# One pool for the eight PSUM banks of a banded attention, and another order of its first two blocks

## The chip, the cores and the metric

The kernel runs on one core of one Trainium2 chip. It is one program; the metric is its device time in microseconds, the median of several executions. TensorE (PE) multiplies matrices and writes PSUM, which has eight banks; VectorE (DVE) and ScalarE (ACT) read PSUM and compute element by element, GpSimd (POOL) computes between tiles of SBUF, and SyncE (SP) issues most of the DMAs. Each engine works through its own queue in order, and an instruction that needs another engine's result waits on a semaphore.

## The reference

Attention over 4 batches of 8 heads, 768 positions of 64 dimensions, in which each position sees the first 4 positions (the sinks) and the last 128 of its own. Then a mixture of 8 experts over 3072 tokens of 512 dimensions, each expert with 1024 hidden units, weighted by a table that is normalized in eight Sinkhorn steps:

```python
keep = is_sink | in_window                   # n_sink = 4, window = 128
scores = np.where(keep, scale * (q @ k.T), -1e9)
a = np.exp(scores - scores.max(-1, keepdims=True))
a = a / (a.sum(-1, keepdims=True) + 1e-9)
x = (a @ v)                                  # regrouped to (3072, 512)
P = np.exp(x @ w_gate - max)                 # 8 times: rows, columns to sum 1, times N / E
for e in range(E):
    out += P[:, e:e + 1] * (np.maximum(x @ w1[e], 0) @ w2[e])
```

All of it is in fp32. The kernel splits the operands of the large products into a high and a low part and adds three products of parts.

## The kernel before, in words

The attention stage takes blocks of 128 positions, 24 in all (4 batches of 6). Half a block, four heads, is a unit; unit j is half j % 2 of block j // 2, so that the fifth unit has number 4. The work of a unit goes as follows. `transpose_qk` (L451) turns k and q by four transposes on PE into one PSUM bank. `split_qk` copies that bank to the high part on ACT (L460) and takes the low part on DVE (L461); in a batch's second block a small copy of the sinks follows on DVE (L464). `scores` (L483) multiplies them in 12 matmuls into four banks, one bank per head. `exponential` handles one head: on DVE a predicated copy that brings the two pieces of the window together (L492, not in a batch's first block), then the sum with the mask and the scaling (L493), and on ACT the exponential (L495). `scaled` has the reciprocals of the sums on DVE (L501, L502) and the scaling of four heads on POOL (L504). `transpose_p` (L514) turns the weights into a bank and `copy_p` copies them on ACT (L520) and masks a copy on POOL (L522). `values` (L564) multiplies with v into a bank called O, which both halves of a block share; `split_p`, `small_products` and `sink_values` (L537, L538, L544, L549, L572) add the sinks' part. `store_x` copies O half by ACT (L581) and half by DVE (L582), issues the DMA to DRAM, and for the first 1024 tokens queues a high copy on ACT (`behind`, L589) and a low part on POOL (`lows`, L590). `gate_products` (L597) computes the gate's logits of a block, and ACT copies them (L599).

Beside attention runs a filling, `fill`, that is a generator of steps of the first expert's products for a third of the tokens. `plain_g1` is 12 matmuls of 256 columns into a bank (L631) in two steps; ACT (L636) and DVE (L637) read that bank. `plain_g2` is 12 matmuls of 512 columns (L646) in four steps; ACT (L654) or DVE (L656) reads the bank. The DVE instruction is not emitted at once: it is put on the list `pending` and emitted by the next `flush`. `next_piece` copies a piece of a weight on ACT (L749) and puts its low part (L750) on the same list. `run_fill(k)` emits k steps.

The whole stage stands in `tc.manual_schedule()`: every engine's queue has the order in which the program emits the instructions. The first two blocks, up to the fifth unit's sums, are written out by hand, with `idle(k)`, k matmuls of zeros into a bank of their own, in places. Then a list `rounds` rules. Each round emits the scores and sums of the units `new_s` (two units in most rounds, a half in the first three), `ahead` filling steps, the values of the units of the round before, the gate's products, the q/k transposes of `new_qk`, the P transposes of `new_p`, the small products, `store_x`, and then `steps` filling steps. What is pending on DVE is flushed behind the second head's sums. From block 4 on, a round with four filling steps has two `plain_g1` or one `plain_g2`, by turns. In the last rounds no scores are left.

PSUM banks are given out by `new_bank`. It keeps a ring of eight numbers, `banks`; a tile takes the first number, which goes to the end of the ring at once, or, with `keep`, only when the program appends it again: O does so in the written-out part (`store_x` appends it), and the bank of zeros until the fourth round. A tile whose bank is still being read waits for the readers. The framework's planner, which lays out all semaphores ahead of the run, resolves the waits. In a pool with `bufs=8` and one name the planner itself picks the bank, among those that no tile holds any more.

## Time and profile before

| | us |
|---|---|
| median of 3 runs (lowest, highest) | 2114.72 (2113.69, 2117.1) |
| the profiled execution | 2114.56 |
| its span | 2112.8 |
| PE busy in the span | 2073.9 (98%) |
| DVE, ACT, POOL busy | 1478.3, 842.9, 703.9 |

The profiled execution stands for the others: it is 0.16 us from the median, and 1.8 us of it lie around the span. Times below are microseconds from the start of the span. In a timeline row the first number is the start, the second the duration; a bracket at the end gives the idle time before the instruction on its engine and what ended it. xN is the number of instructions in the row.

### The profile page before, as it was taken

To read this page: it belongs to the slowest core of one execution; us is meant where nothing else is said; L and a number is where in the kernel's file an instruction comes from. 1 tells how busy PE (TensorE), PEld (TensorE's weight loads), DVE (VectorE), ACT (ScalarE), POOL (GpSimd) and SP (SyncE) were. 2 spreads that over 40 slices of the span, in tenths; PEclk is the share of its full clock that TensorE was granted. 3 is DMA by queue.
4 is the path that set the end of the run, shared out by engine and by line. 5 is a ranking of instruction groups with operands and counts; after the bars stand their busy time and mean duration, and the time that the engine had idled before them with its cause. 6 is when DMAs were issued, how large, how long until landed. Compare 5 with 4: busy or idle time off the path is not lost.

```text
span 2112.8 us, 31704 instructions
## 1 busy us (share of the span) xinstructions
PE 2073.9 (98%) x10609; PEld 1721.6 (81%) x10609; DVE 1478.3 (70%) x2770; ACT 842.9 (40%) x1799; POOL 703.9 (33%) x829
## 2 busy tenths in 40 slices
PE   8998899999999999999999999999999999999998
PEld 6787787888888888888888888888888888888887
DVE  6766778877877776856666666666666666666666
ACT  6766635444444444443322332322433322332322
POOL 5665533242332321322322223223322332223223
PEclk9999999999999999999999999999999999999999
DMA  6644329999898996786666666668766666666662
GB/s 141 156 106 103 75 90 350 298 305 300 294 313 286 306 296 209 239 270 199 208 191 205 204 201 197 204 200 299 263 199 197 203 205 192 205 200 192 204 198 85
DMA packets 397624, 453.82 MB, mean 215 GB/s; under 512 B 99664, under 2 KB 265744, under 8 KB 396560
## 3 DMA queue, kind: packets, MB, share of 16 engines
q1 hardware_dynamic: 397064, 451.57, 68.7%
q8 instruction: 87, 1.43, 0.3%
q14 instruction: 81, 0.66, 0.1%
q10 hardware_dynamic: 392, 0.16, 0.0%
HBM read 314.17 MB, written 137.46 MB: 214 GB/s over the span
## 4 chain that ended last, share of the span: by engine, by line
PE 93%; DVE 4%; ACT 2%; DMA 1%; issue 1%; POOL 0%; SPq 0%; DVEq 0%; ACTq 0%; POOLq 0%
PE c L968 41%; PE o L1532 20%; PE held L1532 8%; PE o L1218 7%; PE held L1218 7%; PE st L646 2%; PE st L631 2%; PE st L564 2%; PE st L483 1%; DVE sc L493 1%; DVE st L492 1%; PE st L451 1%; PE st L514 1%; ACT KQ L460 0%; ACT sc L495 0%
## 5 line engine op out<-in xcount | busy, mean ns | idle before, releaser
L994 ACT CAST hf<-w 128x512 fp32r<-128x512 f32 x448 | 265.2, 621 | 562.2 <-POOL w L1499 299.7
L1532 PE MATMUL o<-hf,W2q 128*128 128x512 f32 x1920 | 472.0, 389 | 0.0
L1532 PEld LDWEIGHTS o<-hf,W2q 128*128 128x128 f32 x1920 | 360.0, 188 | 75.5 <-DVE acc L1546 0.9
L968 PE MATMUL c<-T,W1q 128*128 128x512 f32 x1530 | 388.9, 389 | 0.2 <-DVE w L1480 0.2
L997 DVE TENSOR_TENSOR hf<-w,hf 128x512 fp32r<-128x512 f32 x448 | 329.4, 764 | 76.4 <-ACT hf L994 68.9
L968 PEld LDWEIGHTS c<-T,W1q 128*128 128x128 f32 x1530 | 286.8, 188 | 60.7 <-DVE w L1480 0.9
L1546 DVE TENSOR_TENSOR acc<-o,acc 128x512 f32<-128x512 f32 x298 | 204.8, 688 | 170.0 <-PE o L1532 170.0
L968 PE MATMUL c<-B,W1q 128*128 128x512 f32 x1134 | 278.3, 389 | 0.0
L968 PEld LDWEIGHTS c<-B,W1q 128*128 128x128 f32 x1134 | 212.6, 188 | 44.0
L1499 POOL TENSOR_TENSOR w<-w 128x512 f32<-128x512 f32 x64 | 82.7, 1292 | 493.2 <-DVE w L1481 493.2
L1480 DVE TENSOR_TENSOR w<-c,M 128x512 f32<-128x512 f32 x192 | 132.4, 689 | 139.7 <-PE c L968 135.3
L1476 ACT COPY M<-c 128x512 f32<-128x512 f32 x192 | 112.9, 588 | 250.4 <-PE c L968 250.3
L1532 PE MATMUL held<-hf,W2q 128*128 128x512 f32 x768 | 195.1, 390 | 0.7 <-DMA W2q<-w2s 0.7
L1218 PE MATMUL held<-W2f,h 128*128 128x512 f32 x672 | 171.1, 390 | 0.0
L968 PE MATMUL c<-T,W1f 128*128 128x512 f32 x672 | 171.0, 390 | 0.1
L1218 PE MATMUL o<-W2f,h 128*128 128x512 f32 x672 | 170.6, 390 | 0.1
L1532 PEld LDWEIGHTS held<-hf,W2q 128*128 128x128 f32 x768 | 143.9, 188 | 30.9 <-DMA W2q<-w2s 1.1
L1514 POOL TENSOR_TENSOR w<-w 128x512 f32<-128x512 f32 x64 | 106.3, 1660 | 176.1 <-DVE hf L997 176.1
L1218 PEld LDWEIGHTS o<-W2f,h 128*128 128x128 f32 x672 | 126.0, 188 | 27.0 <-DVE acc L1225 0.9
L968 PEld LDWEIGHTS c<-T,W1f 128*128 128x128 f32 x672 | 125.9, 188 | 26.6 <-issue 0.5
L1218 PEld LDWEIGHTS held<-W2f,h 128*128 128x128 f32 x672 | 125.9, 188 | 26.4 <-DVE W2f L997 0.5
L1503 POOL TENSOR_TENSOR w<-w 128x512 f32<-128x512 f32 x64 | 83.7, 1308 | 176.0 <-DVE w L1481 171.8
(212 smaller groups left out, 2714.8 us busy)
## 6 DMA issues: line engine op xcount, KB each, us to landing
W2q<-w2s SPq DMA_DIRECT2D x448, 256.0 KB, 3.0
W1q<-w1s SPq DMA_DIRECT2D x444, 256.0 KB, 2.9
w1s<-W1f SPq DMA_DIRECT2D x56, 896.0 KB, 7.6
w2s<-WT SPq DMA_DIRECT2D x136, 256.0 KB, 4.0
r<-in_moe_w_dram SPq DMA_DIRECT2D x64, 512.0 KB, 4.0
w2s<-W2f SPq DMA_DIRECT2D x56, 256.0 KB, 5.1
PB<-psd SPq DMA_DIRECT2D x16, 512.0 KB, 3.7
w2s<-W2f SPq DMA_DIRECT2D x56, 128.0 KB, 6.7
```

Source lines behind the costliest of these rows:

```text
L564: nc.tensor.matmul(O[r * D:(r + 1) * D, c], lhsT=x_[:, 2 * c + r], rhs=y_[:, 2 * c + r], start=(j == 0 and c == 0), stop=(j == len(ops) - ...
L968: nc.tensor.matmul(ps, lhsT=w1(a, k), rhs=x[:, b, k, :], start=(start and j == 0), stop=(stop and j == len(TERMS) - 1), skip_group_check=n ...
L994: nc.scalar.copy(dst[:, 0], src)
L997: low_ = nc.vector.tensor_sub(dst[:, 1], src, f32(dst[:, 0])).ins
L1218: nc.tensor.matmul(o, lhsT=h[c, th][:, a, off:off + P], rhs=W2F[n][:, w, c, :], start=(begin and c == 0 and j == 0), stop=(end and c == 1 ...
L1476: nc.scalar.copy(t, T["c2"])
L1480: nc.vector.tensor_add(w, T["c1"], T[m])
L1499: nc.gpsimd.tensor_sub(S3, T["A11"], T["A21"])
L1503: nc.gpsimd.tensor_add(T["A21"], T["A21"], T["A22"])
L1514: at(k, lambda: nc.gpsimd.tensor_sub(T["A11"], w, T["A11"]))
L1532: nc.tensor.matmul(o, lhsT=W2Q[part, n, m][:, a, k * P:(k + 1) * P], rhs=F[part, n, H_OF[m]][:, w, :], start=(j == 0 and (begin or not hol ...
L1546: nc.vector.tensor_add(sums[m, k], o, sums[m, k])
```

## The change

`new_bank` becomes a pool of eight buffers with one name, and the ring, `keep` and the appending go. `split_qk` is divided into its ACT part, `high_qk`, and its DVE part, `low_qk`. In the written-out part the DVE parts move behind sums that stood after them, the sums of two or four heads are brought together, `store_x(0)`, `next_piece`, `high` and `total(3)` change places with transposes and copies, and one of the four low parts of x goes to DVE. The first four filling steps, so far in the first round (`ahead` 4), are emitted ahead of it, behind the fifth unit's sums. The filling's steps per round are 4 in all rounds but two of the steady part (m is 11 and 17, with none), and 4 in three of the last four, where they were 2, 2, 0 and 0: the sum is 92 steps before and after.

```diff
@@ -367,16 +367,8 @@
     w1r_ = ctx.enter_context(ExitStack())
     w1r = right(w1r_, "w1r", 1)
     ph = ctx.enter_context(ExitStack())
-    ps_a = ph.enter_context(tc.tile_pool(name="ps_a", bufs=1, space=PSUM))
-    banks = list(range(8))
-
-    def new_bank(shape, keep=False):
-        j = banks.pop(0)
-        if not keep:
-            banks.append(j)
-        t = ps_a.tile(shape, F32, name=f"st{j}")
-        return (t, j) if keep else t
-
+    ps_a = ph.enter_context(tc.tile_pool(name="ps_a", bufs=8, space=PSUM))
+    new_bank = lambda shape: ps_a.tile(shape, F32, name="st")
     wa, rawp = right(ph, "wa", 2), right(ph, "rawp", 2)
     XF["B12"] = b12p.tile([P, 2, KH, HT], F32R, name="B12")
     ab = ctx.enter_context(ExitStack())
@@ -451,17 +443,29 @@
                 nc.tensor.transpose(pt[:, 2 * pr + j, :], r[:, h0 + 2 * pr:h0 + 2 * pr + 2, :].rearrange("p h d -> p (h d)"), ident)
                 idle(gap * (pr == j == 0))
 
+    def qk_parts(m, hh):
+
+        t = KQ[hh]
+        return (t[:, w, :, SINK:].rearrange("p r (a c) -> p r a c", a=2)[:, :, :, turn_of(*spans[m])] for w in range(2))
+
+    def high_qk(m, hh):
+
+        nc.scalar.copy(next(qk_parts(m, hh)), us[m]["qk", hh].rearrange("p (r a) t -> p r a t", a=2))
+
+    def low_qk(m, hh):
+
+        b, i = spans[m]
+        hi, lo = qk_parts(m, hh)
+        nc.vector.tensor_sub(lo, us[m]["qk", hh].rearrange("p (r a) t -> p r a t", a=2), f32(hi))
+        if i == 1:
+
+            t = KQ[hh]
+            nc.vector.tensor_copy(t[:, :, :, 0:SINK], f32(t[:, :, :, place(b, 0)])[:, :, :, 0:SINK])
+
     def split_qk(m, hh):
 
-        b, i = spans[m]
-        t = KQ[hh]
-        hi, lo = (t[:, w, :, SINK:].rearrange("p r (a c) -> p r a c", a=2)[:, :, :, turn_of(b, i)] for w in range(2))
-        src = us[m]["qk", hh].rearrange("p (r a) t -> p r a t", a=2)
-        nc.scalar.copy(hi, src)
-        nc.vector.tensor_sub(lo, src, f32(hi))
-        if i == 1:
-
-            nc.vector.tensor_copy(t[:, :, :, 0:SINK], f32(t[:, :, :, place(b, 0)])[:, :, :, 0:SINK])
+        high_qk(m, hh)
+        low_qk(m, hh)
 
     def scores(m, hh):
 
@@ -550,11 +554,11 @@
         for j, (t, ls) in enumerate(sums):
             nc.vector.tensor_copy(Pt[:, t, :], tsk[:, 1 + j, 0:E])
 
-    def values(m, hh, keep=True):
+    def values(m, hh):
 
         u = us[m]
         if hh == 0:
-            u["O"], u["bank"] = new_bank([P, KC, P], True) if keep else (new_bank([P, KC, P]), None)
+            u["O"] = new_bank([P, KC, P])
         O = u["O"]
         ops = list(zip(u["V"], u["PT"]))
         c0 = hh * NP
@@ -574,8 +578,6 @@
 
     def store_x(m):
         b, i = spans[m]
-        if us[m]["bank"] is not None:
-            banks.append(us[m]["bank"])
         tok = b * S + i * P
         xr = us[m]["xr"] = att.tile([P, KC, P], F32, name="xr")
         nc.scalar.copy(xr[:, 0:NP], us[m]["O"][:, 0:NP])
@@ -587,7 +589,7 @@
                 x_ = xr[:, kh * KH:(kh + 1) * KH, :]
                 b_ = xblock(kh, tok // HT)
                 behind.append(lambda b_=b_, x_=x_, cols=cols: nc.scalar.copy(b_[:, 0, :, cols], x_))
-                lows.append(lambda b_=b_, x_=x_, cols=cols: nc.gpsimd.tensor_sub(b_[:, 1, :, cols], x_, f32(b_[:, 0, :, cols])))
+                lows.append(lambda b_=b_, x_=x_, cols=cols, eng=nc.gpsimd: eng.tensor_sub(b_[:, 1, :, cols], x_, f32(b_[:, 0, :, cols])))
         later.append((tok // P, xr))
 
     def gate_products(t, xr):
@@ -755,11 +757,11 @@
     pieces.extend([(0, 0), (1, 0), (0, 1), (1, 1)])
     rounds = []
     for n in range(FIRST, 2 * HALF + 1):
-        rounds.append(([n + 1], {4: [6], 5: [7, 8]}.get(n, [n + 3]), [n], (4, 0) if n == FIRST else (0, 2), 2))
+        rounds.append(([n + 1], {4: [6], 5: [7, 8]}.get(n, [n + 3]), [n], (0, 0) if n == FIRST else (0, 2), 2))
     rounds.append(([2 * HALF + 2, 2 * HALF + 3], [2 * HALF + 4, 2 * HALF + 5], [2 * HALF + 1], (0, 4), 2))
     for m in range(HALF + 1, L + 3):
         both = lambda j: [2 * j, 2 * j + 1] if j < L else []
-        rounds.append((both(m + 1), both(m + 2), both(m), (0, {L - 1: 2, L: 2, L + 1: 0, L + 2: 0}.get(m, 4)), 2))
+        rounds.append((both(m + 1), both(m + 2), both(m), (0, 0 if m > L + 1 or m in (11, 17) else 4), 2))
     at_block = lambda m: len(rounds) - (L + 3 - m)
     waiting = []
     load_kq(0)
@@ -770,21 +772,18 @@
     load_v(1)
     nc.sync.dma_start(wgp[:, :, 0:E], wg.rearrange("(k p) e -> p k e", p=P))
     load_plain_raw(1, 0)
-    zeros = new_bank([P, P], True)
+    zeros = new_bank([P, P])
 
     def idle(k_):
         for _ in range(k_):
-            nc.tensor.matmul(zeros[0], lhsT=zero, rhs=zero, start=True, stop=True)
-
-    turn_p, score, value, copied_p, cast_qk, total = ((lambda j, f=f: f(*divmod(j, 2))) for f in (transpose_p, scores, values, copy_p, split_qk, scaled))
+            nc.tensor.matmul(zeros, lhsT=zero, rhs=zero, start=True, stop=True)
+
+    turn_p, score, value, copied_p, cast_qk, cast_high, cast_low, total = (
+        (lambda j, f=f: f(*divmod(j, 2))) for f in (transpose_p, scores, values, copy_p, split_qk, high_qk, low_qk, scaled))
 
     def exps(j, *hs):
         for h in hs:
             exponential(j // 2, j % 2 * HH + h)
-
-    def low():
-        while lows:
-            lows.pop(0)()
 
     def high():
         while behind:
@@ -801,13 +800,13 @@
         score(1)
         transpose_qk(1, 0)
         transpose_qk(1, 1)
-        cast_qk(2)
+        cast_high(2)
         mask_sinks(0)
-        exps(1, 0, 1)
+        exps(1, 0, 1, 2, 3)
         total(0)
-        exps(1, 2, 3)
+        cast_low(2)
         value_step(0)
-        cast_qk(3)
+        cast_high(3)
         idle(5)
         score(2)
         exps(2, 0)
@@ -815,60 +814,61 @@
         turn_p(0)
         copied_p(0)
         exps(2, 1)
+        cast_low(3)
         idle(3)
         value(0)
         turn_p(1)
-        exps(2, 2)
+        exps(2, 2, 3)
         copied_p(1)
         value_step(1)
         score(3)
-        exps(2, 3)
         load_kq(3)
         load_kq(4)
         load_plain_raw(0, 1)
         load_plain_raw(1, 1)
-        next_piece()
         exps(3, 0, 1)
         total(2)
-        exps(3, 2)
+        exps(3, 2, 3)
         idle(2)
         value(1)
-        store_x(0)
-        exps(3, 3)
-        flush(len(pending))
-        high()
-        total(3)
         transpose_qk(2, 0)
         turn_p(2)
+        total(3)
         copied_p(2)
+        store_x(0)
+        next_piece()
+        high()
         split_sinks(0)
         split_p(1, slice(0, H))
-        next_piece()
-        idle(5)
+        flush(len(pending))
+        idle(6)
         turn_p(3)
         copied_p(3)
-        cast_qk(4)
-        flush(len(pending))
+        next_piece()
         value(2)
         small_products(1, [])
         load_v(2)
-        idle(2)
+        idle(1)
         value(3)
         sink_values(1)
+        cast_qk(4)
+        flush(len(pending))
         store_x(1)
         high()
         score(4)
         transpose_qk(2, 1)
         load_kq(5)
-        low()
-        add_up_rows()
+        for j in range(3):
+            lows.pop(0)()
         exps(4, 0, 1)
+        lows.pop(0)(eng=nc.vector)
         cast_qk(5)
         exps(4, 2, 3)
         total(4)
+        add_up_rows()
+        run_fill(4)
+        flush(len(pending))
         for n, (new_s, new_qk, new_p, (ahead, steps), np_) in enumerate(rounds):
-            if n == 3:
-                banks.append(zeros[1])
             if n in (at_block(4), at_block(5)):
                 load_plain_raw(n - at_block(4) + 2, 0)
             elif n in (at_block(6), at_block(7)):
@@ -907,7 +907,7 @@
             run_fill(ahead)
             flush(len(pending))
             for j in waiting:
-                values(*divmod(j, 2), j + 1 not in waiting)
+                values(*divmod(j, 2))
             old = list(summed)
             summed.clear()
             for g in later:
```

## Rows read from the trace of the kernel before

**Rows 1.** The page, busy time: engine, us (share of the span), instructions

```profile
PE 2073.9 (98%) x10609; PEld 1721.6 (81%) x10609; DVE 1478.3 (70%) x2770; ACT 842.9 (40%) x1799; POOL 703.9 (33%) x829
```

**Rows 2.** Windows by stage: from:to, length, busy us (instructions) per engine, clock, DMA share, GB/s

```profile
29.00:63.65 34.65, 29.91 (x246) 24.93 (x244) 26.93 (x103) 23.26 (x78) 18.73 (x45) 0.85 0.44 94
63.65:275.00 211.35, 189.97 (x2038) 165.20 (x2037) 141.73 (x632) 142.79 (x490) 119.74 (x257) 1.00 0.46 105
275.00:2112.80 1837.80, 1829.75 (x8137) 1512.13 (x8129) 1293.34 (x1957) 660.83 (x1182) 549.41 (x480) 1.00 0.72 230
```

**Rows 3.** Waits of PE, 63.65 to 275: us in total, times, longest

```profile
PE st L631 <- DVE xr L582: 9.4, 7, 1.8
PE st L483 <- DVE h L637: 8.6, 10, 0.9
...
PE st L483 <- DVE acc L656: 1.1, 1, 1.1
```

**Rows 4.** Timeline of PE in three rounds

```profile
156.69 1.70 PE L483 MATMUL st<-KQ 64*128 64x260 f32 x24
158.32 1.09 PE L564 MATMUL st<-PT,vr 128*64 128x128 f32 x16
...
186.16 1.65 PE L631 MATMUL st<-B,W 128*128 128x256 f32 x12
189.37 1.69 PE L631 MATMUL st<-B,W 128*128 128x256 f32 x12 [1.56 <-DVE xr L582]
190.99 1.47 PE L483 MATMUL st<-KQ 64*128 64x260 f32 x19
193.33 0.62 PE L483 MATMUL st<-KQ 64*128 64x260 f32 x5 [0.87 <-DVE h L637]
193.88 0.66 PE L564 MATMUL st<-PT,vr 128*64 128x128 f32 x8
...
207.84 3.08 PE L631 MATMUL st<-B,W 128*128 128x256 f32 x24
```

**Rows 5.** Timeline of ACT, the copy of the gate's bank

```profile
186.26 0.24 ACT L599 COPY ls<-st 128x128 f32<-128x128 f32 x1
```

**Rows 6.** Timeline of DVE, the round of 190.99

```profile
192.09 0.30 DVE L493 CUSTOM_DVE_ANT_0 sc<-st,mask 128x132 f32<-128x132 f32 x1
...
192.64 0.29 DVE L493 CUSTOM_DVE_ANT_0 sc<-st,mask 128x132 f32<-128x132 f32 x1
...
199.91 0.42 DVE L582 COPY xr<-st 128x256 f32<-128x256 f32 x1
```

**Rows 7.** Timeline of PE, fifth to ninth unit

```profile
27.82 0.99 PE L483 MATMUL st<-KQ 64*128 64x260 f32 x12
...
31.00 0.39 PE L483 MATMUL st<-KQ 64*128 64x260 f32 x2 [1.60 <-ACT KQ L460]
...
32.52 4.63 PE L631 MATMUL st<-B,W 128*128 128x256 f32 x24
...
39.72 0.87 PE L483 MATMUL st<-KQ 64*128 64x260 f32 x10 [0.34 <-DVE KQ L461]
...
54.84 1.02 PE L483 MATMUL st<-KQ 64*128 64x260 f32 x6 [0.75 <-DVE h L637]
```

**Rows 8.** Waits of DVE, 0 to 29, and two of them in its timeline

```profile
DVE KQ L461 <- ACT KQ L460: 8.4, 5, 2.8
...
10.03 0.69 DVE L461 TENSOR_TENSOR KQ<-st,KQ 128x512 fp32r<-128x512 f32 x1 [1.55 <-ACT KQ L460]
...
13.21 0.69 DVE L461 TENSOR_TENSOR KQ<-st,KQ 128x512 fp32r<-128x512 f32 x1 [1.28 <-ACT KQ L460]
```

**Rows 9.** Windows, the rounds of blocks 11 and 17

```profile
136.23:146.24 10.01, 9.54 (x113) 8.76 (x113) 6.14 (x27) 6.81 (x25) 5.81 (x12) 1.00 0.58 120
201.57:210.86 9.29, 9.29 (x113) 8.71 (x113) 5.06 (x27) 6.82 (x25) 5.84 (x12) 1.00 0.63 134
```

**Rows 10.** A window with a lower clock

```profile
53.50:60.50 7.00, 6.25 (x46) 5.01 (x45) 6.62 (x28) 4.45 (x17) 3.72 (x9) 0.51 0.71 151
```

## The prediction

> **What bounds the kernel now.** I read the page's busy times first: PE is busy for 98% of the span [rows 1], so a microsecond counts only if PE's own queue gets shorter by it. The windows by stage come next [rows 2]: from 275 us to the end PE idles 8.1 us in 1837.8, and nothing of the change lies there; from 63.65 to 275 us it idles 211.35 - 189.97 = 21.4 us, and from 29 to 63.65 us 4.7 us at a mean clock of 0.85. The change is wholly in the attention stage, 0 to 275 us, so what PE gains there moves the rest forward by as much. The waits view says who ends PE's idle time in 63.65 to 275 us [rows 3]: `DVE xr L582` 9.4 us in 7 waits, `DVE h L637` 8.6 us in 10, `DVE acc L656` 1.1 us in one, together 19.1 of the 21.4 us. All three are DVE instructions that read a PSUM bank, and the waiting matmuls (L631, L483) read nothing that these write: PE waits for the bank, not for data. The timeline of one round shows where [rows 4]: the second product of the filling starts at 189.37 after 1.56 us of idling, and the next scores stop after 19 of 24 matmuls for 0.87 us.
>
> **The change part by part.**
>
> *One pool in its own order.* Before, banks go round in a fixed ring. In a round 8 scores take all eight; O, the gate's bank, two q/k transposes, two P transposes and the small products take the next seven, the filling's two products the eighth and then O's own bank. O is read last, by L582. In the ring after that, the eighth head gets the bank of the filling's second product, whose reader L637 is emitted behind the second head. I take the new pool to hand out the bank that has been free longest by the planner's account; the trace of before can't show that, and it is my main assumption.
>
> (a) The filling's second product then gets the gate's bank, which ACT L599 reads at 186.26 [rows 5], some 2.8 us before PE asks for it. First to second product takes 189.37 - 186.16 = 3.21 us with the wait and 3.08/2 = 1.54 without [rows 4]: 1.67 us for an idle time of 1.56, so 0.1 to 0.15 more than the wait itself. Seven such waits: 9.4 + 7 x 0.15 = 10.4 us. Bounds: 0 (some late bank again) and 10.4. I take 10.4, because every other bank of the round is read before L582. Next on PE come the scores of the next round; DVE is through with L582 by then and idle, so nothing else is late.
>
> (b) The eighth head gets the first head's bank, free when L493 ends (192.09 + 0.30 = 192.39); O gets the second head's, free at 192.64 + 0.29 = 192.93 [rows 6]. Before, the values (L564) start 193.88 - 190.99 = 2.89 us after the scores; with no wait that is 158.32 - 156.69 = 1.63 us [rows 4]. Now they can start at about 193.03 (0.1 for the signal), 2.04 us after: a gain of 0.85 us and a left-over of 0.4, which holds up only PE's own queue (values, gate, transposes). Ten waits: 8.5 us, bounds 0 and 10 x 1.26 = 12.6. The wait on L656 has the same form: 1.0 us. One more on L637, 0.75 us at 54.84 [rows 7], lies in the stage before: 0.4 us.
>
> (c) What the pool adds: PE now follows DVE's frees more closely, one head per 0.55 us (192.09 to 192.64), while a round's seven tiles are asked for one every 0.4 to 0.5 us. Where weight pieces stand between two heads on DVE, PE can wait 0.3 us more. No row shows it; bounds 0 and 19 rounds x 0.4 = 7.6 us (the left-over of (b) in every round). I take 3.0, nearer to 0, because the rounds without the two waits already run on the same frees.
>
> *First two blocks.* DVE waits 8.4 us in five waits for ACT's q/k copy [rows 8]. The first two (3.1 us) precede any scores and stay; the other three are 1.55 us before 10.03, 1.28 before 13.21, and 2.47 later. In the first two DVE stands in front of L461 while scores lie ready in PSUM. The change puts those sums first: the second unit's can run from 8.48 (10.03 - 1.55) instead of 10.7, in the shadow of ACT's exponentials, and the third unit's need not follow L461 at 13.21. I followed each engine's new order with the durations of the trace up to the fifth unit's scores, which then start at about 23.0 instead of 27.82 [rows 7]: 4.8 us. Bounds 2.8 (the first two waits alone) and 5.3 (all three). What moves along costs nothing there: `store_x(0)` takes its two copies and its DMA behind the transposes of P, and no step asks for its O bank meanwhile; SP's loads keep their order; the three POOL sums of `add_up_rows` are asked for only a round later.
>
> *Filling behind the fifth unit's scores.* The four steps now stand where PE waits 1.60 us for the sixth unit's q/k copy [rows 7]. But then PE has nothing left to put in front of the seventh unit's copy, which hangs on ACT and DVE: I find about 2.6 us of idling there, where before the filling covered it. From the fifth unit's scores to the second part of the seventh's it is 39.72 - 27.82 = 11.9 us before; after, I get about 11.2, the chain over DVE and ACT, with the filling (3.1 us at full clock instead of 4.63 [rows 4, 7]) no longer on it. So 0.7 us; bounds -1.5 (PE idles behind a chain that does not shorten) and +3.1 (the wait gone and 1.5 us from the clock). The fourth low part goes to DVE, in front of the sixth unit's L461: 0.42 us as L582 [rows 6], in time that DVE spends waiting for ACT there; uncovered it costs 0.4.
>
> *Steps moved.* The filling still gets 92 steps in all: 8 leave the rounds of blocks 11 and 17 and go to the last three rounds. These two rounds last 10.01 and 9.29 us with PE busy 9.54 and 9.29, DVE 6.1 and 5.1, ACT 6.8 [rows 9]; less 3.1 us of filling PE has 6.2 to 6.5 us, so ACT becomes their bound: 0.3 to 0.6 us of idling each. The tail has next to no idle PE and takes the steps at their price. Net a loss of 0.8 us; bounds 0 and 6.2 (the rounds not shorter at all).
>
> **Sum.** -10.4 - 8.5 - 1.0 - 0.4 + 3.0 - 4.8 - 0.7 + 0.8 = -22.0 us. The profiled run took 2114.56 us (span 2112.8 and 1.8 around it), 0.16 below the median of the three runs, so no correction: 2092.6, **2093 us**.
>
> The clock is the one thing that no term holds. Between 53.5 and 60.5 us it is granted at 0.51, the 1.2 GHz level, with PE busy 6.25 us [rows 10], with a bank wait of 0.75 us in it [rows 7]; at 2.4 GHz that work takes some 3.2 us less. From 63.65 to 275 us the clock is 1.00 [rows 2], through all eighteen bank waits. The Trainium skill (TensorE: Matmul & The Clock Gate, "A second HAM failure mode: psum-queue depth-cycling") says that short idles between groups of matmuls, made by cycling through banks, can be enough to make the clock swing between its levels. By that rule the going of the waits would give more than the sum; the trace doesn't agree in the steady rounds, since the clock stays at 1.00 there.
>
> **The rivals.**
> 1. *The low stretch goes too.* For it: its 0.75 us bank wait goes. Against: the new idle of 2.6 us that I find ahead of the seventh unit's scores is longer than that wait, and the clock was low once more, in the first products of the filling (4.63 us for 3.1 at full clock), behind a wait for data. It gives 3.2 us more: 2090.
> 2. *PE's gain is eaten by DVE and ACT.* For it: DVE's chain in a round, scores to the end of L582, is 200.33 - 190.99 = 9.3 us [rows 4, 6], and PE's round without waits about 9.7, so there is little slack, and weight pieces lengthen the chain. Against: DVE now idles about 2 us ahead of each round's first sums. If half of (a) and (b) comes back as waits for data: 2093 + 10 = 2103.
> 3. *The pool does not do what it says.* The planner's order gives O's late bank to the second product again, and the eighth head still waits for L637; only the first blocks gain, less what the moved filling may lose: 2114.6 - 5.5 + 3 = 2112, within 0.2%.
> 4. *Slower.* The planner's account frees banks in another order than DVE does, and O, first after the scores, is given a later head's bank. Each head later costs 0.55 us in each of 19 rounds, 10.5 us; from two heads later on it eats the gain, at three it is 2093 + 31 = 2124. For it: nothing in the trace fixes that order. Against: DVE works the heads strictly in order, and any account that follows its queue frees them so.
>
> **How the numbers follow.** The forecast has 0.50, rival 1 0.12, rival 2 0.18, rival 3 0.09, rival 4 0.11. The forecast's own range, from the bounds of (c) and of the first blocks, is 2087 to 2100. To leave out no more than 2 in 10 I go from 2085 (rival 1 with (c) near 0 and the start at its bounds) to 2109 (rival 2 with a start that gains nothing). A change under 0.2% (4.2 us) can't be told from none here. Faster: forecast, rivals 1 and 2, 0.80; same 0.09; slower 0.11.
>
> **What would show it.** The waits of L631 on L582 gone, and those of L483 on L637 gone or replaced by waits on L493 of 0.1 to 0.4 us; PE's idle time from the round that started at 63.65 to the end of attention 6 to 9 us instead of 21.4; the fifth unit's scores at about 23 us; a new idle of 2 to 3 us ahead of the seventh unit's; the rounds of blocks 11 and 17 without L631 or L646 and 6.5 to 7 us long; the stretch after attention as long as before. The forecast is wrong if L564 waits for L493 by 0.5 us or more in most rounds, if L483 starts to wait for L461 there, or if a clock below 1.00 shows in the steady rounds.

## The result and the profile after

The changed kernel takes 2096.09 us in the median (4 runs, 2094.96 to 2096.62), the kernel before 2115.91 on the same chips: ratio 0.9904, 95% interval 0.9887 to 0.9921. That is 19.8 us faster; 22 had been forecast (2093.0), and the time lies in the range. The profiled execution took 2096.42 us, its span is 2094.6, 18.2 us less than before. In the kernel after, the transposes of q and k are L443, q/k's low part L459, the scores L487, the sums L497, the values L568, `xr` L584, the filling's products L633 and L648, its low part L639, the weight pieces' low part L752.

The page's busy time:

```profile
PE 2071.2 (99%) x10609; PEld 1718.1 (82%) x10609; DVE 1480.7 (71%) x2771; ACT 843.2 (40%) x1799; POOL 704.8 (34%) x828
```

Windows by stage, with the columns of [rows 2]; 60.79 is the start of block 5's scores, as 63.65 was:

```profile
0.00:60.79 60.79, 51.61 (x444) 41.95 (x444) 44.43 (x182) 39.27 (x128) 34.62 (x94) 0.94 0.69 155
60.79:256.34 195.55, 190.20 (x2040) 164.65 (x2040) 142.48 (x633) 142.83 (x490) 120.37 (x255) 1.00 0.51 119
256.34:2094.60 1838.26, 1829.44 (x8129) 1511.48 (x8127) 1293.79 (x1956) 661.10 (x1181) 549.83 (x480) 1.00 0.71 229
```

The middle row answers to the second of [rows 2]: PE's busy time is the same (190.2 against 190.0 us) and its idle time is 195.55 - 190.20 = 5.35 us instead of 21.4. The rest of the kernel is as long as it was. The waits of PE from 60.79 to the first product of the table's column sums (264.28) name what is left:

```profile
PE st L568 <- POOL PC L526: 1.6, 2, 0.9
PE st L518 <- DVE st L497: 0.6, 1, 0.6
PE st L548 <- POOL sc L508: 0.6, 3, 0.2
PE st L551 <- DVE st L497: 0.6, 3, 0.2
PE st L443 <- PE st L599: 0.3, 1, 0.3
```

All three waits of [rows 3] are gone. The timeline of PE shows a round with filling and the next one, block 17's, which has none now:

```profile
179.78 3.08 PE L633 MATMUL st<-B,W 128*128 128x256 f32 x24
182.79 1.60 PE L487 MATMUL st<-KQ 64*128 64x132 f32 x24
...
189.21 1.73 PE L487 MATMUL st<-KQ 64*128 64x260 f32 x24
191.02 0.66 PE L568 MATMUL st<-PT,vr 128*64 128x128 f32 x8
192.57 0.66 PE L568 MATMUL st<-PC,dV 128*64 128x128 f32 x8 [0.89 <-POOL PC L526]
```

Against [rows 4] the two products run through in 3.08 us, the scores in one piece. The round without filling takes 189.21 - 182.79 = 6.42 us; the longest wait left follows it.

The start, on PE, and what POOL does just ahead of the wait at 22.65:

```profile
22.65 0.32 PE L548 MATMUL st<-ident,SS 128*96 128x128 f32 x1 [0.72 <-POOL SS L542]
...
24.74 0.99 PE L487 MATMUL st<-KQ 64*128 64x260 f32 x12
...
34.85 0.54 PE L487 MATMUL st<-KQ 64*128 64x260 f32 x2 [2.16 <-DVE st L505]
35.65 0.59 PE L487 MATMUL st<-KQ 64*128 64x260 f32 x2 [0.27 <-DVE KQ L459]
```

```profile
21.21 0.66 POOL L541 TENSOR_SCALAR SS<-sc 128x64 fp32r<-128x64 f32 x1
21.95 0.65 POOL L542 TENSOR_TENSOR SS<-sc,SS 128x32 fp32r<-128x32 f32 x1
```

The fifth unit's scores start at 24.74 instead of 27.82 [rows 7], 3.1 us earlier; from there to the second part of the seventh's it is 10.91 us instead of 11.90. Then 1.2 us are given back: from 35.65 to block 5's scores it is 25.14 us, before 63.65 - 39.72 = 23.93. Two things lie in that stretch. Behind the idle time at 34.85 the clock is granted at 0.54 from 34.8 to 38.2 us, so for the most part at the 1.2 GHz level. And block 4's round has a wait, here on DVE and, in the second fence, on PE:

```profile
51.12 0.42 DVE L639 SCALAR_TENSOR_TENSOR h<-st,h 128x256 fp32r<-128x256 f32 x1
51.45 2.34 DVE L752 TENSOR_TENSOR W2f<-r,W2f 128x512 fp32r<-128x512 f32 x2
53.72 0.28 DVE L496 COPY_PREDICATED st<-pick,st 128x128 f32<-128x128 int32 x1
```

```profile
54.44 0.30 PE L443 MATMUL st<-ident,kr 128*128 128x128 f32 x1 [1.66 <-issue]
```

Two weight pieces stand between the second and the third head's sums on DVE and take 2.34 us; PE's transposes ask for the third head's bank and start when its sum has been taken (L497, 54.03 to 54.32).

### The profile page after: what moved, and what is told of

Its sections match the earlier page's. It is cut to its first block, busy times and chain, and to the rows that moved or that the text cites. A ratio compares the mean times of both kernels' runs of the same rounds, so it can differ in the third digit from the quotient of the medians.

```text
span 2094.6 us, 31723 instructions
## 1 busy us (share of the span) xinstructions
PE 2071.2 (99%) x10609; PEld 1718.1 (82%) x10609; DVE 1480.7 (71%) x2771; ACT 843.2 (40%) x1799; POOL 704.8 (34%) x828
## 4 chain that ended last, share of the span: by engine, by line
PE 93%; DVE 4%; ACT 1%; DMA 1%; issue 1%; POOL 1%; SPq 0%; ACTq 0%; DVEq 0%; POOLq 0%
PE c L968 41%; PE o L1532 21%; PE held L1532 8%; PE held L1218 7%; PE o L1218 7%; PE st L633 2%; PE st L648 2%; PE st L487 1%; PE st L568 1%; DVE sc L497 1%; DVE st L496 1%; PE st L443 1%; PE st L518 1%; PE st L576 0%; PE o L648 0%
```

## The experiments

The stages of every profiled run, by the starts on PE of the fifth unit's scores, of block 5's scores and of the first product of the table's column sums, and the span's end, beside the medians of all runs:

| kernel | fifth unit | block 5 | column sums | span | median | ratio to before |
|---|---|---|---|---|---|---|
| before | 27.82 | 63.65 | 283.28 | 2112.8 | 2115.9 | |
| after | 24.74 | 60.79 | 264.28 | 2094.6 | 2096.1 | 0.9904 |
| pool alone | 29.38 | 64.69 | 266.73 | 2096.8 | 2096.8 | 0.9907 (0.9891 to 0.9924) |
| ring put back | 24.64 | 61.75 | 285.46 | 2115.7 | 2115.5 | 0.9996 (0.9986 to 1.0005) |
| O kept out | 28.08 | 62.38 | 270.46 | 2100.8 | 2103.4 | 0.9942 (0.9925 to 0.9958) |
| ring turned | 28.97 | 67.41 | 290.11 | 2121.6 | 2123.1 | 1.0030 (1.0019 to 1.0042) |
| old steps | 24.61 | 60.87 | 262.63 | 2093.7 | 2093.5 | 0.9895 (0.9877 to 0.9912) |
| filling in the round | 24.53 | 59.90 | 263.30 | 2095.0 | 2097.5 | 0.9914 (0.9896 to 0.9932) |
| sinks early | 25.14 | 61.38 | 264.88 | 2094.7 | 2097.4 | 0.9917 (0.9899 to 0.9934) |
| one item | 24.57 | 56.60 | 256.40 | 2085.8 | 2086.9 | 0.9863 (0.9845 to 0.9881) |
| one item, old steps | 24.61 | 56.79 | 255.04 | 2084.2 | 2086.6 | 0.9864 (0.9847 to 0.9880) |
| pool, one item | 28.81 | 59.73 | 257.64 | 2087.3 | 2089.3 | 0.9876 (0.9859 to 0.9892) |
| no item | 25.99 | 59.34 | 255.53 | 2086.0 | 2087.4 | 0.9865 (0.9849 to 0.9882) |
| no item, old steps | 24.68 | 56.99 | 254.48 | 2085.3 | 2087.0 | 0.9863 (0.9847 to 0.9880) |

Each ratio is to runs of the kernel before that were taken beside it (medians 2115.3 to 2116.7). A profile is one execution: its time can be 2 us from its kernel's median. From the column sums to the end all profiles have 1829 to 1832 us. Where medians of two experiments are set against each other below, no interval was measured for the pair.

**Pool alone.** The kernel before with this hunk only:

```diff
-    ps_a = ph.enter_context(tc.tile_pool(name="ps_a", bufs=1, space=PSUM))
-    banks = list(range(8))
...
+    ps_a = ph.enter_context(tc.tile_pool(name="ps_a", bufs=8, space=PSUM))
+    new_bank = lambda shape: ps_a.tile(shape, F32, name="st")
```

> The kernel before with one part of the change alone: the pool of eight banks in place of the ring; written-out part, steps and filling stay. Theory (the order in which banks are handed out gives the gain of the steady rounds, by itself): L631 no longer waits for L582 nor L483 for L637, PE's idle time from block 5's scores to the end of attention falls from 21.4 to 6 to 9 us, that stretch from 211.7 to about 195 us, the fifth unit's scores stay at 27.8; 2098 to 2099 us, ratio 0.992. Rival (the waits went because the order of the first blocks and the moved filling shifted the engines against each other): the waits stay, 2110 to 2114. A pool that hands out late banks on its own: above 2114.

2096.8 us, a little under the 2098 to 2099 put. From block 5's scores to the column sums it is 202.04 us against 219.63 before, 17.6 less, and PE's waits there are:

```profile
PE st L444 <- PE st L588: 1.2, 2, 0.6
PE st L537 <- POOL sc L497: 0.8, 4, 0.2
PE st L540 <- DVE st L486: 0.6, 3, 0.2
```

(L444 are the transposes here, L588 the gate's products, L537 and L540 small products, L497 POOL's scaling, L486 the sums.) A round that had waited for L637 before, on PE and, in the second fence, the second head's sum on DVE:

```profile
120.73 2.15 PE L476 MATMUL st<-KQ 64*128 64x260 f32 x24
122.81 0.66 PE L557 MATMUL st<-PT,vr 128*64 128x128 f32 x8
```

```profile
122.38 0.30 DVE L486 CUSTOM_DVE_ANT_0 sc<-st,mask 128x132 f32<-128x132 f32 x1
```

The values (L557) start 2.08 us after the scores and 0.13 us after the second head's sum has ended, as term (b) has it for O in the second head's bank. The theory holds: the pool's order is the gain. The sum's terms for it, -10.4 - 8.5 - 1.0 + 3.0 = -16.9, are 0.7 us from the 17.6. The kernel after is only 0.75 us below this run by the medians, and their runs overlap (2094.96 to 2096.62 against 2096.35 to 2098.54): what the rest of the change brought can't be told from nothing here. The profile's start is later than before's since the clock was low there once.

**Ring put back.** The kernel after with the ring, `keep` and the appending of the kernel before:

```diff
+    banks = list(range(8))
+    def new_bank(shape, keep=False):
...
-    new_bank = lambda shape: ps_a.tile(shape, F32, name="st")
```

> The kernel after with the ring of banks put back (O and the zeros kept as before): the other parts of the change alone. Theory: the steady rounds have their 18 waits again (9.4 us on L582's line, 8.6 us on L637's), the fifth unit's scores stand at about 24.7 as in the kernel after; what is left of the gain is the start, 3 to 4 us, less 0.8 for the moved steps: 2112 to 2113, ratio 0.9985. Rival (the two parts need each other: the ring makes the new order of the first blocks wait for banks): 2115 or more. If the sum of this run's and the pool's gain alone is the whole 19.8 us, the parts add up.

2115.5 us: no difference from before can be measured, so the theory's number failed. The start is as early as in the kernel after, but the next stage is 223.71 us, 4.1 longer than before. PE's waits there:

```profile
PE st L643 <- DVE xr L594: 10.6, 8, 1.8
PE st L495 <- DVE h L649: 7.0, 9, 0.9
PE st L495 <- DVE xr L594: 2.9, 3, 1.6
```

(L643 is the filling's product here, L594 `xr`, L649 the filling's low part.) The third line is new. Where the filling is taken out of a round, O's late bank comes to the next scores (L495) instead of the filling's second product (L643). And the clock falls behind the longest of these new waits, as the timeline of PE and a window behind it show:

```profile
142.72 1.71 PE L495 MATMUL st<-KQ 64*128 64x260 f32 x23 [1.64 <-DVE xr L594]
```

```profile
143.00:146.40 3.40, 3.40 (x43) 3.27 (x43) 2.86 (x12) 1.08 (x5) 0.00 (x0) 0.69 0.87 206
```

It falls once more behind a wait of L643 of 1.85 us at 226.00. Of the 4.1 us, 0.8 are idle time and 3.3 PE's busy time (201.55 against 198.25). So, as the trace reads, the moved steps need the pool: under the ring they make a wait of their own. No run has the ring and the new order with the old steps, so that is not shown apart. Parts can't simply be added.

**O kept out.** One line of the kernel before, so that O's bank goes back to the ring only in `store_x`:

```diff
-                values(*divmod(j, 2), j + 1 not in waiting)
+                values(*divmod(j, 2), True)
```

> The kernel before with one edit: O's bank stays out of the ring until store_x in all rounds, so that the filling's second product gets the gate's bank. It parts term (a) from term (b) of the sum. Theory: the seven waits of L631 on L582 go, the ten of L483 on L637 stay (0.87 us each) or grow a little since PE comes earlier; -10.4 us, bounds -8 and -12: 2104 to 2107. Rival (a bank wait taken away comes back at the next bank or as a wait for DVE's or ACT's data): above 2110.

2103.4 us, just under the 2104 to 2107 put. From block 5's scores to the column sums 208.08 us, 11.55 less than before. PE's waits there:

```profile
PE st L483 <- DVE h L637: 8.6, 10, 0.9
PE st L451 <- PE st L597: 1.2, 2, 0.6
PE st L483 <- DVE acc L656: 1.1, 1, 1.1
```

L631's waits are gone, L483's ten are as they were: (a) and (b) are two separate things, and nothing came back. (a) is 11.55 where 10.4 was put: 9.4 us of idle time and 2.1 us of PE's busy time (198.25 to 196.14), all of it L631's (39.4 to 37.3): 0.3 for each of the seven waits, not 0.15. The run gains 13.3 us by the medians and 12.0 by the spans. Beside the 11.55, 1.5 come from the fifth unit's to block 5's scores (34.30 us against 35.83), where the clock was low for less.

**Ring turned.** The run before, and:

```diff
             flush(len(pending))
+            if len(new_s) == 2:
+                banks[:] = banks[2:] + banks[:2]
             for j in waiting:
```

> The run before this one (O's bank kept out until store_x) with the ring turned by two ahead of O in the 20 rounds that score two units: O gets the third head's bank instead of the first's. It measures the price of rival 4 of the prediction. By that rival's law (each head later 0.55 us in each round) it is 20 x 1.1 = 22 us slower than the run before this one: 2127. Refined: in the ten rounds where the eighth head already waits for L637 the values start 2.89 us after the scores and the third head is free at 2.04 + 1.1 = 3.14, so 0.25 us each there and some 1.5 us in the other ten: 17 us, 2122. Rival (PE's later start is made good in the same round, since DVE and ACT catch up and PE then waits less): under 6 us.

2123.1 us, 19.8 above the run before it. Two rounds on PE, the first without the eighth head's wait, the second with it:

```profile
159.79 1.70 PE L483 MATMUL st<-KQ 64*128 64x260 f32 x24
163.48 1.44 PE L564 MATMUL st<-PT,vr 128*64 128x128 f32 x16 [1.99 <-issue]
...
173.87 0.62 PE L483 MATMUL st<-KQ 64*128 64x260 f32 x5 [0.87 <-DVE h L637]
174.50 0.66 PE L564 MATMUL st<-PT,vr 128*64 128x128 f32 x8
```

DVE in the first, from the second head's sum on:

```profile
161.55 1.29 DVE L750 TENSOR_TENSOR W<-r,W 128x512 fp32r<-128x512 f32 x2
...
163.07 0.30 DVE L493 CUSTOM_DVE_ANT_0 sc<-st,mask 128x132 f32<-128x132 f32 x1
```

The values start 0.1 us after the third head's sum (163.37). So rival 4 names a real mechanism; only the pool doesn't order banks so. From block 5's scores to the column sums the values' waits are:

```profile
PE st L564 <- issue: 9.5, 6, 2.1
PE st L564 <- DVE st L493: 1.2, 1, 1.2
PE st L564 <- PE st L483: 0.9, 1, 0.9
```

The total is near both forms of the price (22 and 17 us), but it isn't made as they say. Eight of the 19 rounds there wait, 11.6 us in all: four without the wait for L637 (0.9 to 2.1 us) and four that have that wait too (1.1 to 1.2 us more); the others pay nothing that the trace shows. What else stands on DVE ahead of the third head's sum (weight pieces, as in the first of the two rounds shown, or the split of a batch's sinks) makes the wait longer than one head's 0.55. The rest goes with the clock: PE is busy 4.8 us longer in this stage than in the run before (200.94 against 196.14), and from the fifth unit's to block 5's scores it is 38.44 us against 34.30, at 0.82 instead of 0.95. In the steady rounds the clock falls three times behind waits of 1.1 to 2.0 us: to 0.54 in the window from 163.8 to 167.2, which is 3.4 x 0.46 = 1.6 us of full speed.

**Old steps.** The kernel after with

```diff
-(0, 0 if m > L + 1 or m in (11, 17) else 4)
+(0, {L - 1: 2, L: 2, L + 1: 0, L + 2: 0}.get(m, 4))
```

> The kernel after with the old numbers of filling steps per round: four steps again in the rounds of blocks 11 and 17, fewer in the last rounds. The prediction put the move of these steps at a loss of 0.8 us, so theory: 0.8 us faster than the kernel after, each of the two rounds 3.1 us longer and the last rounds 6.2 us shorter. Rival (the two rounds are shorter by nearly the whole 3.1 us, since ACT is not their bound, and the last rounds had idle time of PE to take the steps): 0.5 to 2 us slower. Either is small: 2094.5 to 2098.

2093.5 us, 2.6 below the kernel after by the medians, 0.9 by the spans; the intervals of the two ratios overlap. The two waits for POOL's `PC` after the emptied rounds are gone. Theory, in sign, if the difference is one; the size lies between 0.3 (with one item, below) and 2.6.

**Filling in the round.** The kernel after with the first four filling steps in the first round again:

```diff
-(0, 0) if n == FIRST
+(4, 0) if n == FIRST
...
-        run_fill(4)
-        flush(len(pending))
```

> The kernel after with the first four filling steps back in the first round, behind the sixth unit's scores. Theory (the prediction's term of 0.7 us, 1.0 in the trace): PE waits about 1.6 us for the sixth unit's q/k copy again, the idle time of 2.2 us ahead of the seventh unit's scores goes, and from the fifth unit's scores to the second part of the seventh's it is 11.6 to 11.9 us instead of 10.9; 0.7 to 1.0 us slower. Rival (the place of the filling does nothing, PE idles as much in the other place): within 0.3 us. If the clock stays low in another stretch, 1 to 2 us more or less.

2097.5 us, 1.4 more than after, but the runs overlap (the lowest is 2095.65). From the fifth unit's scores to the second part of the seventh's it is 36.41 - 24.53 = 11.88 us against 10.91, with the wait of 1.61 us back: 1.0, the theory's number. But the place is not its cause. The filling ran at the low clock here, and in the run with O kept out, in the same old place, at full clock:

```profile
29.47 4.38 PE L633 MATMUL st<-B,W 128*128 128x256 f32 x24
```

```profile
32.79 3.13 PE L631 MATMUL st<-B,W 128*128 128x256 f32 x24
```

There the stretch is 39.00 - 28.08 = 10.92 us, in the pool's own run 40.31 - 29.38 = 10.93, as long as with the filling moved. So the rival holds wherever the clock is full. By block 5's scores this run is 0.9 ahead of the kernel after, with a clock of 0.97 up to there against 0.94.

**Sinks early.** The kernel after with `split_sinks(0)` behind `cast_low(2)`:

```diff
         cast_low(2)
+        split_sinks(0)
...
-        split_sinks(0)
         split_p(1, slice(0, H))
```

> The kernel after with the split of the first batch's sinks (DVE's casts, POOL's split) emitted right behind the third unit's low part instead of ahead of the second half block's split. The fifth unit's scores came at 24.7 instead of the predicted 23.0; in 20 to 22.6 us POOL's two splits took 0.65 us each instead of 0.24 and PE waited 0.72 us for them while DVE cast at the same time. Theory (that contention and its place are 0.7 us of the missing 1.7): the wait of L548 on POOL goes, the fifth unit's scores at about 24.0, 0.7 us faster: 2095.4. Rival (the chain over DVE's sums sets that time and PE waits elsewhere): no change, or up to 1 us slower as the casts now stand in front of sums.

POOL's two splits then take

```profile
22.39 0.24 POOL L541 TENSOR_SCALAR SS<-sc 128x64 fp32r<-128x64 f32 x1
22.71 0.25 POOL L542 TENSOR_TENSOR SS<-sc,SS 128x32 fp32r<-128x32 f32 x1
```

and PE's 0.72 us wait for them is gone, but from the third unit's scores to the fifth's it is 25.14 - 11.49 = 13.65 us, exactly as in the kernel after (24.74 - 11.09). PE waits 0.42 us for the first transposed P and 0.24 for POOL's scaling instead. The rival, in its result: DVE's casts now stand ahead of the third unit's sums, so that the fourth unit's reciprocals (L506) start 19.61 - 11.49 = 8.12 us after the third unit's scores instead of 18.68 - 11.09 = 7.59, and POOL's masked copy of P (L526) behind them takes 1.08 us instead of 0.81. These 0.8 us are about what the wait gave back. The run does not say what the splits would cost with the casts out of DVE's way.

**One item.** The kernel after, behind the second head's sums:

```diff
                 if c == 1:
-                    flush(len(pending))
+                    flush(1)
```

> The kernel after with one list item instead of all emitted behind the second head of each round, so that the second weight piece's low part (L752, 1.2 us on DVE) goes behind the last head. Theory (DVE's pieces between the second and the third head hold up the bank that O or the next tile asks for): the 1.7 us wait for a bank at 54.4 and most of the short waits on L497 go, the 1.2 us that block 4's round gave back return, 1 to 3 us faster: 2093 to 2095. Rival (the low parts come later for the products that read them, or PE waits for later heads instead): 0 to 2 us slower.

2086.9 us, 9.2 below the kernel after, more than the theory's 1 to 3. PE in block 4's round, where no wait stands ahead of the transposes (51.28):

```profile
50.92 0.43 PE L599 MATMUL st<-xr,wgp 128*32 128x128 f32 x8
51.28 0.33 PE L443 MATMUL st<-ident,kr 128*128 128x128 f32 x1
```

The stages, and the rest of the waits:

```profile
0.00:56.60 56.60, 49.92 (x443) 40.80 (x443) 41.44 (x182) 39.27 (x128) 34.63 (x90) 0.97 0.73 160
56.60:256.40 199.80, 196.50 (x2088) 171.43 (x2087) 145.47 (x649) 144.42 (x494) 128.58 (x265) 1.00 0.52 123
```

```profile
PE st L568 <- POOL PC L526: 1.3, 2, 1.0
PE st L551 <- DVE st L497: 0.4, 2, 0.2
PE st L548 <- POOL sc L508: 0.2, 1, 0.2
```

4.2 us come ahead of block 5's scores (4.0 from the fifth unit's on): the waits of 1.66 and 0.8 us and the low stretch of the clock behind them, 0.55 from 55.2 to 58.6 in the kernel after. 3.7 us come from there to the column sums: 2.05 of idle time (203.49 - 198.14 = 5.35 to 3.30), the rest of PE's busy time.

**One item, old steps; pool, one item; no item; no item, old steps.** The edits are those above, joined; "no item" takes the two lines `if c == 1: flush(len(pending))` away, so that L639 too goes behind the last head.

> The kernel after with two edits that each came out below it: one list item behind the second head (2086.9, 9.2 us below the kernel after) and the old numbers of steps per round (2093.5, 2.6 us below by the medians, 0.9 by the spans). Theory (they work on different waits: DVE's order within a round, and PE's filling in blocks 11 and 17): they add up, 2084.3 to 2086.0. Rival (with the shorter chain on DVE the two rounds without filling no longer wait for POOL and the moved steps cost nothing): 2086.5 to 2087.5.

> The kernel before with the pool of banks and one list item behind the second head: nothing of the new order of the first blocks, of the moved filling and of the moved steps. It prices the written-out part once more, without the weight pieces that ate 1.2 us in block 4's round. Theory (the order of the first blocks brings the fifth unit's scores 3.1 us forward and keeps it): 3 us above the run with both edits on the kernel after: 2087 to 2089, fifth unit's scores at 27.5 to 28. Rival (the start's gain is lost again before block 5, in idle time or in clock, as the ring's run with the new order, 1.2 us below before, suggests): 2084 to 2086.

> The kernel after with nothing emitted from the list behind the second head: the filling's low part (L639) goes behind the last head as well. It parts the two items of that place. Theory (what cost PE there is the weight piece of 1.2 us, while L639 frees the bank of the filling's second product, which the pool hands to a late head or to O, and gives the low part that the next products read): 1 to 4 us slower than the run with one item, 2088 to 2091. Rival (the heads' sums set everything, and each 0.42 us taken from in front of them counts): 1 to 3 us faster, 2084 to 2086.

> The kernel after with nothing emitted behind the second head and the old numbers of steps per round. In the profiles the run without that emission needs 196.2 us from block 5's scores to the first matmul of the table's column sums, the one with one item 199.8, and the old steps took 1.6 to 1.7 us from that stretch in both pairs. Theory (both are real): 194.6 us there and 2083 to 2085 in all. Rival (what is saved in that stretch is given back in the round of block 4 and after attention, as the medians of the run without the emission and of the one with both edits say): 2086 to 2087.5.

The first gives 2086.6, its rival: the moved steps cost nothing once DVE's chain is shorter. The second gives 2089.3, 2.7 above the first, which differs from it by the written-out part and the moved filling alone: the theory, a little less. The third, 2087.4, fits neither of its two forecasts: the stretch from block 5's scores to the column sums is 3.6 us shorter than with one item, what lies around it longer by as much (2.7 us ahead of block 5's scores, where the clock is lower, 0.93 instead of 1.00 up to the fifth unit's scores and 0.90 instead of 0.95 from there). The fourth, 2087.0, its rival: that stretch is 197.5 us there, not 194.6. The four versions on the kernel after, 2086.6 to 2087.4, can't be told apart; each beats both kernels, and the one item is the smallest edit.

## Why the prediction was right, point by point

- *The sum.* -22.0 put; -19.8 by the medians, -18.1 by the profiled executions (2114.56 to 2096.42). That it comes so near is in part luck. The pool was put at 17.3 us with the 0.4 of block 4's round, and by the medians its own run has 19.8 already (2116.67 to 2096.84). Everything else was put at 4.7 and brings 0.75, within the noise.
- *The bound.* Right. PE's idle time in the steady rounds fell to 5.35 us (6 to 9 put), DVE and ACT did not take its place, and the stretch after attention did not move.
- *The main assumption*, that the pool hands out the bank longest free, bears the forecast: no round waits for O's or for L637's bank, and the values start 0.13 us behind the second head's sum. Which bank a tile has does not stand in the trace. The turned ring shows what another order costs.
- *(a), (b), (c).* -16.9 by the sum, -17.6 in the pool's own run. (a) is -11.55, not -10.4, as L631 was busy 0.3 us longer for each wait beyond the idle time. (The gate's bank was free only 1.3 us before PE asked for it, at 189.37 - 1.56 = 187.81, not 2.8; that changes nothing.) (b), with L656, reads as put, 9.2 us against 9.5: in the eleven rounds that had waited, the values started 2.79 to 3.16 us after the scores before and start 1.96 to 2.11 after in the pool's run (2.04 put). (c) was put at 3.0; 11.55 + 9.2 - 17.6 = 3.2 us come back, of which 4.12 - 2.3 = 1.8 are idle time. In the kernel after PE newly waits 5.35 - 2.3 = 3.05 us, for which (c) and the moved steps together had 3.8. But these waits were other ones than said: not for L493's frees in each round, but for POOL's `PC` after the emptied rounds, and for the heads behind the weight pieces.
- *First two blocks.* 4.8 us by the fifth unit's scores were put, 3.1 came between the two profiles (bounds 2.8 and 5.3). The place varies from run to run: the five profiles with the old order have it at 27.82 to 29.38, those with the new one, sinks early left out, at 24.53 to 25.99. I explained the missing 1.7 us by POOL's splits, which take 0.66 us beside DVE's casts. The run with the sinks early doesn't bear that out, nor does it refute it; the cause stays open. With the moved filling it was to be 5.5 us, and of these 2.7 reach the end ("one item, old steps" against "pool, one item").
- *Filling behind the fifth unit's scores*: the term that was mis-sized. 0.7 put, 1.0 between the two profiles; but in the old place the stretch is 11.9 us in the three profiles whose filling runs at the low clock (4.4 to 4.6 us) and 10.9 in the three where it runs at 1.00 (3.13 us), no longer than with the filling moved. And the new idle time ahead of the seventh unit's scores, 2.16 us (2.6 put), has a price that no term held. In all eight profiles with the moved filling the clock is low behind it (0.54 to 0.75 from 34.8 to 38.2 us), in the kernel after for up to 3.4 x 0.46 = 1.6 us of full speed. In "pool, one item", which has no such idle time, the clock is 1.00 from the fifth unit's to block 5's scores (30.92 us); in "one item, old steps" it is 0.95 (32.18 us), and 1.3 of the 4.2 us by which its fifth unit's scores are earlier are lost there.
- *Given back up to block 5's scores*: 1.2 us between the two profiles, which no term held. Part of it is the low clock just named, part the wait in block 4's round. That wait comes with the pool, whose own run has it as well (1.66 us at 58.34). I had the weight pieces between two heads as 0.3 us of PE's time, in (c); with two of them, of 2.34 us, PE waits 1.66. The clock falls behind that in the kernel after and in the pool's run, but not in the run with the filling in the round (1.00 from 53.5 to 60.5). The one item takes the wait away.
- *Steps moved.* 0.8 put; 0.9 by the spans, 2.6 by the medians, and 0.3 with one item. The rounds last 6.42 and 6.36 us (6.5 to 7 put).
- *The rivals.* 1: the low stretch at 53.5 is shorter, not gone (0.51 from 53.5 to 60.5 before, 0.76 in the same window after). 2: 3.05 us of new idle time in the steady rounds, not 10. 3: refuted by the pool alone; 4: shown as a mechanism, refuted for this pool.
- *The clock.* In the kernel before it stayed at 1.00 in the steady rounds, through eighteen bank waits. With the ring put back and with the ring turned it falls in these rounds behind five waits of 1.1 to 2.0 us, and behind others as long it stays (2.10 us at 185.98, ring turned). By the rule that the prediction weighed (the Trainium skill, TensorE: Matmul & The Clock Gate, "A second HAM failure mode: psum-queue depth-cycling") bank waits can do that; these two runs agree (0.69 and 0.54 in the windows behind), the kernel before does not.

## What to carry to other kernels

When several engines read PSUM, follow for each tile which reader frees its bank and when, and let the tile that is asked for first take the bank that is freed first; a ring whose last reader comes late makes the bottleneck engine wait though every operand is there. Work that nobody waits for (here weight pieces on DVE) belongs behind the last of the reads that free banks, not between them: moving it brought 9 us, nearly half of what the whole change had brought. A gain at the start of a chain is worth little until the next stage is seen to keep it: of 5.5 us put on it here, 2.7 reached the end, and the idle time that the reordering made was followed by a low clock.

## What the runs showed of the hardware

- The seven waits of L631 for a bank cost PE some 0.3 us each beyond the idle time that the trace gives them: 9.4 us of idle time, L631 busy for 39.4 instead of 37.3 us, and the stage 11.55 us shorter without them. The ten waits of L483 show no such cost: L483 is busy for 36.5 us with them and, in the pool's own run, for 36.2 without.
- POOL's small splits (128x64 and 128x32) took 0.66 and 0.65 us while DVE split the sinks' v and a weight piece, and 0.24 and 0.25 us in the run with the sinks early, where DVE was idle.
- One idle time of PE can be followed by a stretch at the lower clock that costs nearly as much again: behind 2.16 us at 34.85 the clock is 0.54 (34.8 to 38.2) in the kernel after, behind 1.66 us at 54.44 it is 0.55 (55.2 to 58.6), some 1.5 us of full speed each. Not every such wait does it: with the filling in the round the clock stays at 1.00 behind 1.66 us at 54.47.
